# First stage of an attention and two-layer feed-forward kernel: pooled sums by TensorE, another split of one value load, another program order

## The chip, the cores and the metric

The kernel runs on one core of a Trainium2 chip. The metric is the device time of one execution in microseconds (us). Before the change it is 943.6 us, the median of three runs (943.38 to 944.88). The execution that was profiled took 947.2 us.

## What is computed

Inputs are `q`, `k`, `v` of shape (4, 8, 576, 64) in float32 and four weight matrices in float64. Cut to what matters:

```python
q_d, k_d, v_d = means of 4 neighbouring rows (576 -> 144 rows)
out_d = softmax(q_d @ k_d.T / 8) @ v_d             # pooled attention, each row used 4 times
scores = q @ k.T / 8, only where |i - j| < 4       # local attention, 7 keys for a query
out = repeat(out_d, 4) + softmax(scores) @ v       # then to (2304, 512)
h = x @ w_in;  x = (h - tanh(h)) @ w_out           # 512 -> 2048 -> 512
h = x @ w_in2; out = (h * cos(h)) @ w_out2
```

## The kernel before, in words

The 2304 tokens are cut into chunks: rows 0 to 511 of each of the four batches are one chunk of 512 tokens, the last 64 rows of all batches together are one of 256. The second batch's chunk is taken as two halves of 256 tokens ("second chunk" below is the first half). The first feed-forward layer runs chunk by chunk (`ffn1`): sixteen steps, in each twelve matmuls x @ w_in (L744) and, two steps later, twelve matmuls with w_out (L764). The second layer follows with all five chunks. Each factor of a matmul is held as a high and a low half, so a product is three matmuls.

The weights come as float64 and are turned into float32 pairs on the chip. This is one *tick* of the class `Weights`: two ScalarE steps (L121, L123), one VectorE step (L127), a copy for the high half (GpSimd for the first three pieces, ScalarE then) and a GpSimd subtraction for the low half (L142). Each tick also issues the load of a further piece on SP, into a buffer that an earlier tick's VectorE step gives free. The first chunk needs 32 pieces, two for each of its sixteen steps.

There are two kinds of attention. The first chunk's is written for TensorE (`first_attention`): keys and queries are loaded in four tiles of 128 rows each (`load_nat`), transposed (`tr`), and from the transposed tiles VectorE makes the sums of four neighbours (`red`). The same is done for the last 64 rows of all batches (`load_lo`, `tr_l`, 'left-over' rows). Local scores are worked in eight blocks of 64 queries: scores (`b_s`), maximum, subtraction and exponential (`b_m`), sum and division (`b_n`), transposition (`b_t`), then products with the values (`b_v`) and the low half of the result (`b_l`). A value block is 70 rows (`load_vw`); the first begins three rows ahead of the sequence. The pooled attention runs in four pairs of heads (`P.s`, `P.e`, `P.n`, `P.t`, `P.t2`, `P.v`); the sums of its values are `vsum` on GpSimd. After nearly every TensorE step a matmul on zeros is issued (`warm`, L359).

The other chunks' local attention (`attention`) is elementwise: GpSimd multiplies (L553 for queries with keys, L602 for values), VectorE reduces. Their pooled attention shares the class `Pooled`; its keys need a copy of left-over rows on GpSimd (L261).

Order. Every step of the attention and every tick is an event with a key (a time in a plan). The events up to `T0` are written out in the order of their keys, and each engine works its instructions in just this order. After `T0` the events are handed out along the feed-forward loop (5.2 units of the plan for a step of a 512-token chunk), and a planner arranges the instructions. `TB` is the plan time at which the second chunk's attention begins, `TL` the earliest of its loads, `TS` the distance of two of its products. Weight ticks stand at `TE + 2.3 * i` for the first `KE` and after that from `T0` on at a distance of `TW`. In the plan before the first stage's steps have fixed distances: tiles every 2.5, score blocks every 3.1, pooled pairs every 2.2; six ticks and three products of the second chunk lie among the stage's last steps.

Of the kernel before, what the change touches and what calls it, by code (L numbers as in the profile page):

```python
# [27 lines left out]
def kernel(  # L28
# [11 lines left out]
    nc = tc.nc  # L40
# [18 lines left out]
    def pool(name, bufs=1, **kw):  # L59
        return tc.tile_pool(name=name, bufs=bufs, **kw)  # L60
# [5 lines left out]
    ps_h = ctx.enter_context(pool("ps_h", 2, space=PS))  # L66
    ps_a = ctx.enter_context(pool("ps_a", 2, space=PS))
# [5 lines left out]
    lp = st_lp.enter_context(pool("lp"))  # L73
# [91 lines left out]
    ident = ao.tile([128, 128], F32, name="ident")  # L165
# [3 lines left out]
    klq = cst.tile([128, 2, NP, 64], F32, name="klq")  # L169
    vl = cst.tile([128, DM], F32, name="vl")  # L170
# [159 lines left out]
    def first_attention(ch):  # L330
# [37 lines left out]
        def rows_of(src, b, t0, n):  # L368
            return src[b, :, t0:t0 + n, :].rearrange("h s d -> s h d")
# [16 lines left out]
        def load_vw(i):  # L386
            t = lp.tile([NK, H, D], F32, tag="g", name="vw", bufs=12)
            G["vw", i] = t
            a0 = NQ * i - (R - 1)
            z = max(0, -a0)  # L390
            nc.sync.dma_start(out=t[z:NK], in_=rows_of(v, 0, a0 + z, NK - z))
            if z:
                nc.sync.dma_start(out=t[0:z], in_=rows_of(v, 0, 0, z))

        def masks():
            nc.vector.memset(zero, 0.0)
            nc.gpsimd.memset(mask, 0.0)
# [12 lines left out]
            warm(10)  # L410

        def turn_nat(g):
            a = ps_a.tile([128, NP, 128], F32, tag="a", name="pa_tr")
            for u in range(NP):
                nc.tensor.transpose(a[:, u, :], g[:, 2 * u:2 * u + 2, :].rearrange("p e d -> p (e d)"), ident)
            return a

        def tr(nm, t):
            a = turn_nat(G.pop((nm, t)))
            if nm == "q":  # L420
                nc.scalar.activation(qT[:, :, 128 * t:128 * t + 128], a, AF.Copy, scale=0.125)
            else:
                nc.vector.tensor_copy(kT[:, :, R - 1 + 128 * t:R - 1 + 128 * t + 128], a)

        def red(nm, t):
            src, w, o, dst = (qT, 512, 0, qd) if nm == "q" else (kT, 512 + 2 * (R - 1), R - 1, kd)
            nc.vector.tensor_reduce(out=dst[:, :, 32 * t:32 * t + 32],
                                    in_=view(src, [[w, NP], [R, 32], [1, R]], off=o + 128 * t), axis=AX.X, op=ALU.add)

        def tr_l(nm, j):  # L430
            a = turn_nat(G.pop((nm, "l", j)))
            nc.vector.tensor_reduce(out=klq[:, 0 if nm == "k" else 1, :, 32 * j:32 * j + 32],
                                    in_=view(a, [[128, NP], [R, 32], [1, R]]), axis=AX.X, op=ALU.add)
            if (nm, j) == ("k", 0):
                nc.vector.tensor_copy(kT[:, :, 512 + R - 1:512 + 2 * (R - 1)], a[:, :, 0:R - 1])
            if nm == "q":
                ql = klq[:, 1, :, 32 * j:32 * j + 32]
                nc.scalar.activation(ql, ql, AF.Copy, scale=0.125 / (R * R))

        def pooled_qk():  # L440
# [72 lines left out]
        for t in range(NT_):
            keyed += [(0.1 + 0.01 * t, (load_nat, "k", t)), (0.105 + 0.01 * t, (load_nat, "q", t))]
            keyed += [(4.6 + 2.5 * t, (tr, "k", t)), (5.6 + 2.5 * t, (red, "k", t)), (5.8 + 2.5 * t, (tr, "q", t)), (7.2 + 2.5 * t, (red, "q", t))]
        keyed += [(14.7, (tr_l, "k", 0)), (15.9, (tr_l, "q", 0)), (16.8, pooled_qk), (32.0, (tr_l, "k", 1)), (32.9, (tr_l, "q", 1))]
        keyed += [(19.0 + 0.6 * n, x) for n, x in enumerate(vsums)]
        for u in range(NP):
            t0 = 17.4 + 2.2 * u
            keyed += [(t0 + dt, (fn, u)) for dt, fn in ((0, P.s), (1.3, P.e), (3.9, P.n), (5.5, P.t), (6.7, P.t2))]  # L520
            keyed += [(max(t0 + 8.4, 23.0 + 2.4 * u), (P.v, u))]
        for i in range(NB):
            t0 = 8.1 + 3.1 * i
            keyed += [(0.4 + 0.01 * i, (load_vw, i))]
            keyed += [(t0 + dt, (fn, i)) for dt, fn in ((0, b_s), (1.2, b_m), (3.7, b_n), (6.0, b_t))]
        for j in range(NB // 2):
            keyed += [(33.2 + 1.8 * j, (b_v, j)), (35.1 + 1.8 * j, (b_l, j))]
# [282 lines left out]
    W1, W2 = Weights(w_in1, w_out1), Weights(w_in2, w_out2)  # L810
# [174 lines left out]
```

## Time and profile before

| | |
|---|---|
| median of three runs | 943.6 us |
| profiled execution | 947.2 us |
| its span | 945.4 us |
| TensorE busy | 905.0 us, 96% |
| VectorE busy | 577.9 us, 61% |
| ScalarE busy | 480.6 us, 51% |
| GpSimd busy | 402.7 us, 43% |
| mean granted TensorE clock | 0.981 |

Engines in the rows: PE is TensorE, PEld its weight loads, DVE VectorE, ACT ScalarE, POOL GpSimd, SP SyncE, which issues most of the loads. A timeline row gives start and length in us, engine, source line, operation, output and inputs, the count of merged instructions, and in brackets how long the engine stood idle before it and what ended that. Matmuls are pipelined, so lengths overlap and starts are the better measure.

### The profile page before, as it was taken

How to read it: one execution, taken by the hardware profiler on the slowest of the kernel's cores; microseconds unless marked ns; L12 is line 12 of the kernel's file. 1: busy time of each engine (PE TensorE's matmuls, PEld its weight loads, DVE VectorE, ACT ScalarE, POOL GpSimd, SP SyncE). 2: the span in 40 equal slices, each digit the busy share in tenths (PEclk: the TensorE clock that was granted, in tenths of full speed). 3: DMA queues.
4: the chain of work that ended last, by engine and by line, in shares of the span. 5: the costliest groups of instructions: out<-in, count | busy, mean ns of one | idle time of the engine just before them, and what ended most of it. 6: DMA issues, size and time to landing. Idle time of an engine off the chain costs nothing.

```text
span 945.4 us, 13574 instructions
## 1 busy us (share of the span) xinstructions
PE 905.0 (96%) x4922; PEld 748.9 (79%) x4930; DVE 577.9 (61%) x964; ACT 480.6 (51%) x1012; POOL 402.7 (43%) x432
## 2 busy tenths in 40 slices
PE   7859999799998999999999989999999999999997
PEld 4537777599997777778889968888888888888896
DVE  6588777888879862663225576546545554545463
ACT  3658786333433344274227886535544454445464
POOL 3579899889888871540004533101111111111010
PEclk9979999799999999999999999999999999999999
DMA  9688654522323131172014731010101010100000
GB/s 179 120 270 306 218 172 135 159 79 87 98 93 98 40 94 35 34 226 87 1 62 133 227 118 64 1 45 0 45 1 45 1 45 0 45 23 1 23 23 23
DMA packets 65939, 81.73 MB, mean 86 GB/s; under 512 B 21966, under 2 KB 46548, under 8 KB 65872
## 3 DMA queue, kind: packets, MB, share of 16 engines
q1 hardware_dynamic: 64544, 76.01, 27.2%
q0 software_dynamic: 1232, 4.72, 1.5%
q8 instruction: 39, 0.64, 0.3%
q14 instruction: 28, 0.23, 0.1%
q10 hardware_dynamic: 96, 0.13, 0.1%
HBM read 71.40 MB, written 9.44 MB: 86 GB/s over the span
## 4 chain that ended last, share of the span: by engine, by line
PE 73%; DVE 8%; ACT 8%; DMA 6%; issue 2%; POOL 2%; ACTq 0%; DVEq 0%; POOLq 0%
PE h L744 35%; PE oacc L901 21%; PE acc L764 14%; DMA raw<-in_moe_w_out_dram 4%; DMA raw<-in_moe_w_in_dram 2%; DVE wf L127 1%; ACT raw L123 1%; ACT pe L280 1%; DVE o L606 1%; ACT wp L121 1%; PE pa_x L639 1%; DMA qt<-in_q_dram 1%; PE pa_s L269 1%; POOL pr L602 1%; ACT wf L121 1%
## 5 line engine op out<-in xcount | busy, mean ns | idle before, releaser
L901 PE MATMUL oacc<-o,i 128*128 128x512 f32 x864 | 209.8, 392 | 3.3 <-ACT i L751 2.7
L744 PE MATMUL h<-xh,i 128*128 128x512 f32 (+1 forms) x768 | 206.8, 346 | 1.7 <-ACT xh L498 1.6
L764 PE MATMUL acc<-gh,o 128*128 128x512 f32 (+1 forms) x768 | 200.9, 342 | 5.7 <-ACT gh L755 5.7
L744 PE MATMUL h<-x2h,i 128*128 128x512 f32 (+1 forms) x640 | 193.2, 369 | 0.0
L901 PEld LDWEIGHTS oacc<-o,i 128*128 128x128 f32 x864 | 160.8, 188 | 39.3 <-ACT i L751 4.0
L916 POOL TENSOR_SCALAR y<-y 128x512 f32<-128x512 f32 (+1 forms) x80 | 46.8, 584 | 327.9 <-ACT y L914 315.4
L744 PEld LDWEIGHTS h<-xh,i 128*128 128x128 f32 x768 | 137.0, 195 | 19.1 <-issue 2.5
L764 PEld LDWEIGHTS acc<-gh,o 128*128 128x128 f32 x768 | 133.5, 190 | 23.2 <-ACT gh L755 7.3
L744 PE MATMUL h<-xl,i 128*128 128x512 f32 (+1 forms) x384 | 133.1, 347 | 3.5 <-DVE xl L502 3.3
L553 POOL TENSOR_TENSOR pr<-qt,kt 128x896 f32<-128x896 f32 x56 | 119.5, 2145 | 36.1 <-DVE o L606 30.0
L744 PEld LDWEIGHTS h<-x2h,i 128*128 128x128 f32 x640 | 116.7, 188 | 21.7
L764 PE MATMUL acc<-gl,o 128*128 128x512 f32 (+1 forms) x384 | 129.2, 339 | 0.2 <-DVE gl L790 0.2
L744 PE MATMUL h<-x2l,i 128*128 128x512 f32 (+1 forms) x320 | 118.0, 369 | 0.0
L602 POOL TENSOR_TENSOR pr<-vt,s 128x896 f32<-128x896 f32 x56 | 105.2, 1930 | 3.8 <-DVE o L606 1.4
L921 DVE TENSOR_TENSOR h<-h,rr 128x512 f32<-128x512 f32 (+1 forms) x80 | 51.6, 645 | 83.4 <-ACT rr L920 83.1
L919 ACT ACTIVATE rr<-rr 128x512 f32<-128x512 f32 (+1 forms) x80 | 47.1, 588 | 100.7 <-DVE rr L918 100.7
L744 PEld LDWEIGHTS h<-xl,i 128*128 128x128 f32 x384 | 74.7, 195 | 12.2 <-DVE xl L502 4.1
L923 DVE TENSOR_TENSOR i<-h,i 128x512 fp32r<-128x512 f32 (+1 forms) x80 | 50.7, 634 | 48.4 <-ACT i L751 48.3
L764 PEld LDWEIGHTS acc<-gl,o 128*128 128x128 f32 x384 | 72.8, 190 | 8.3 <-DVE gl L790 0.7
L788 DVE TENSOR_TENSOR h<-h,th 128x512 f32<-128x512 f32 x72 | 49.8, 694 | 47.0 <-ACT th L787 46.6
L787 ACT ACTIVATE th<-h 128x512 f32<-128x512 f32 x72 | 42.7, 595 | 66.3 <-PE h L744 66.1
L755 ACT ACTIVATE gh<-h 128x512 fp32r<-128x512 f32 x72 | 42.8, 594 | 65.8 <-PE acc L764 51.8
(171 smaller groups left out, 1243.9 us busy)
## 6 DMA issues: line engine op xcount, KB each, us to landing
raw<-in_moe_w_in_dram SPq DMA_DIRECT2D x32, 512.0 KB
raw<-in_moe_w_out_dram SPq DMA_DIRECT2D x32, 512.0 KB
kt<-in_k_dram SPq DMA_DIRECT2D x16, 320.0 KB
vt<-in_v_dram SPq DMA_DIRECT2D x16, 320.0 KB
kt<-in_k_dram SPq DMA_DIRECT2D x16, 256.0 KB
vt<-in_v_dram SPq DMA_DIRECT2D x16, 256.0 KB
x2l<-x2d POOLq DMA_DIRECT2D x4, 1024.0 KB, 5.6
out_dram<-os SPq DMA_DIRECT2D x16, 256.0 KB
```

The source lines that it names most:

```text
L553: nc.gpsimd.tensor_tensor(out=pr.rearrange("p j f d -> p j (f d)"), in0=view(L["q", h], [[0, OFF], [1, 2 * D]], off=f * D), in1=view(L["k" ...
L602: nc.gpsimd.tensor_tensor(out=pr.rearrange("p f d j -> p j f d"), in0=view(L["v", h], [[D, OFF], [D, 2], [1, D]], off=f * D), in1=view(L[" ...
L744: nc.tensor.matmul(hp[:, i * n:i * n + n], lhsT=wt[:, kk * 128:(kk + 1) * 128], rhs=xt, start=(c == 0), stop=(c == 3 * KD - 1))
L755: nc.scalar.activation(gh, hp, AF.Copy)
L764: nc.tensor.matmul(acc[e], lhsT=wt[:, e * 128:(e + 1) * 128], rhs=gt, start=(f == 0 and i == 0), stop=(f == KF - 1 and i == 2))
L787: it = nc.scalar.activation(th, hp, AF.Tanh)
L788: nc.vector.tensor_tensor(out=hp, in0=hp, in1=th, op=ALU.subtract)
L901: nc.tensor.matmul(acc[t], lhsT=gt[:, t * 128:(t + 1) * 128], rhs=wt, start=(g == 0 and a_ == 0), stop=(g == KF - 1 and a_ == 2))
L916: ip = nc.gpsimd.tensor_scalar(out=y, in0=y, scalar1=-ROUND, scalar2=-TWO_PI_HI, op0=ALU.add, op1=ALU.mult)
L919: nc.scalar.activation(r, r, AF.Abs)
L921: nc.vector.tensor_tensor(out=hp, in0=hp, in1=r, op=ALU.mult)
L923: nc.vector.tensor_tensor(out=G[f][1], in0=hp, in1=G[f][0].bitcast(F32), op=ALU.subtract)
```

## The change

- The sums of four neighbours of keys and queries are made by TensorE, from the tiles as loaded, with a 128 x 32 matrix of ones (`pmat`); VectorE's reductions of the transposed tiles go. The left-over tiles are no longer transposed: the same product gives their sums, with three more columns where three left-over keys are needed as they are.
- The first value block is loaded as 64 + 3 + 3 rows instead of 67 + 3.
- Every step of the first stage has a key of its own. Key and query tiles come in the order 0, 3, 1, 2 and 0, 3, 2, 1; score blocks in the order 0, 4, 1, 2, 3, 5, 7, 6.
- `T0`, `TB`, `TL`, `TS` and `TW` get other values, and two ticks instead of six lie before `T0`.

```diff
+        pmat = lp.tile([128, 32 + R - 1], F32, name="pmat")
...
-            z = max(0, -a0)
-            nc.sync.dma_start(out=t[z:NK], in_=rows_of(v, 0, a0 + z, NK - z))
-            if z:
-                nc.sync.dma_start(out=t[0:z], in_=rows_of(v, 0, 0, z))
+            if a0 >= 0:
+                nc.sync.dma_start(out=t, in_=rows_of(v, 0, a0, NK))
+                return
+            nc.sync.dma_start(out=t[NK - 64:NK], in_=rows_of(v, 0, a0 + NK - 64, 64))
+            for z in (0, R - 1):
+                nc.sync.dma_start(out=t[z:z + R - 1], in_=rows_of(v, 0, 0, R - 1))
...
+            nc.gpsimd.memset(pmat, 1.0)
+            nc.gpsimd.affine_select(out=pmat[:, 0:32], in_=pmat[:, 0:32], compare_op=ALU.is_ge, fill=0.0, base=0,
+                                    pattern=[[-R, 32]], channel_multiplier=1)
+            nc.gpsimd.affine_select(out=pmat[:, 0:32], in_=pmat[:, 0:32], compare_op=ALU.is_ge, fill=0.0, base=R - 1,
+                                    pattern=[[R, 32]], channel_multiplier=-1)
+            nc.gpsimd.tensor_copy(pmat[:, 32:32 + R - 1], ident[:, 0:R - 1])
...
         def tr(nm, t):
-            a = turn_nat(G.pop((nm, t)))
+            g = pairs(G.pop((nm, t)))
+            a = ps_a.tile([128, NP, 128], F32, tag="a", name="pa_tr")
+            for u in range(NP):
+                nc.tensor.transpose(a[:, u, :], g[u], ident)
+            if t == 0:
+                G["p" + nm] = ps_h.tile([128, NP, 128], F32, tag="h", name="pa_p" + nm)
+            for u in range(NP):
+                nc.tensor.matmul(G["p" + nm][:, u, 32 * t:32 * t + 32], lhsT=g[u], rhs=pmat[:, 0:32])
...
-        def red(nm, t):
-            src, w, o, dst = (qT, 512, 0, qd) if nm == "q" else (kT, 512 + 2 * (R - 1), R - 1, kd)
-            nc.vector.tensor_reduce(out=dst[:, :, 32 * t:32 * t + 32],
-                                    in_=view(src, [[w, NP], [R, 32], [1, R]], off=o + 128 * t), axis=AX.X, op=ALU.add)
-
         def tr_l(nm, j):
-            a = turn_nat(G.pop((nm, "l", j)))
-            nc.vector.tensor_reduce(out=klq[:, 0 if nm == "k" else 1, :, 32 * j:32 * j + 32],
-                                    in_=view(a, [[128, NP], [R, 32], [1, R]]), axis=AX.X, op=ALU.add)
+            g = pairs(G.pop((nm, "l", j)))
+            w = 32 + (R - 1) * ((nm, j) == ("k", 0))
+            a = ps_a.tile([128, NP, 128], F32, tag="a", name="pa_trl")
+            for u in range(NP):
+                nc.tensor.matmul(a[:, u, 0:w], lhsT=g[u], rhs=pmat[:, 0:w])
+            if nm == "k":
+                nc.vector.tensor_copy(klq[:, 0, :, 32 * j:32 * j + 32], a[:, :, 0:32])
+            else:
+                nc.scalar.activation(klq[:, 1, :, 32 * j:32 * j + 32], a[:, :, 0:32], AF.Copy, scale=0.125 / (R * R))
...
+        def pooled_k():
+            nc.vector.tensor_copy(kd[:, :, 0:128], G["pk"])
+            nc.gpsimd.tensor_copy(kd[:, :, 128:SG], klq[:, 0, :, 0:LG])
+
+        def pooled_q():
             for e in range(2):
-                nc.scalar.activation(qz[64 * e:64 * e + 64, :, e, :], qd[64 * e:64 * e + 64], AF.Copy, scale=1.0 / (R * R))
+                nc.scalar.activation(qz[64 * e:64 * e + 64, :, e, :], G["pq"][64 * e:64 * e + 64], AF.Copy, scale=0.125 / (R * R))
...
+        keyed = [(-11.11, masks), (-3.58, load_vl), (-2.55, load_vg), (12.23, pooled_q), (14.53, pooled_k), (16.07, load_w)]
+        for fn, nm, ts in (
+                (load_nat, "k", (-27.69, -18.48, -13.36, -19.69)),
+                (load_nat, "q", (-22.4, -10.64, -11.95, -19.31)),
+                (tr, "k", (-11.1, -4.77, 2.45, -8.41)),
+                (tr, "q", (-6.77, 12.12, 7.3, 11.27)),
+                (load_lo, "k", (-3.77, 6.14)),
+                (load_lo, "q", (-6.83, 0.2)),
+                (tr_l, "k", (13.57, 18.81)),
+                (tr_l, "q", (12.22, 24.25)),
...
+                (load_vw, (18, 12.74, 20.51, 8.04, 14.62, 13.87, 2.35, 14.22)),
+                (P.s, (15.3, 16.14, 19.35, 18.3)),
...
+                (P.v, (19.75, 22.51, 27.14, 27.35)),
+                (b_s, (2.69, 14, 16.43, 16.46, 13.22, 20.14, 20.68, 18.44)),
+                (b_m, (12.11, 15.29, 17.52, 19.3, 13.42, 20.16, 22.88, 24.57)),
+                (b_n, (12.13, 17.82, 18.12, 19.36, 16.13, 20.25, 26.44, 25.67)),
...
+                (b_v, (28.77, 29.17, 30.06, 31.28)),
+                (b_l, (30.05, 30.87, 31.42, 31.43)),
...
-    T0, TB, TL = 41.0, 34.0, 31.0
-    TS, TS_POOL, TW = 2.5, 0.9, 1.4
+    T0, TB, TL = 43.42, 38.81, 34.91
+    TS, TS_POOL, TW = 2.57, 0.9, 2.28
...
-    TE, KE = 28.5, 6
+    TE, TD, KE = 27.16, 2.17, 2
...
-        events.append((TE + 2.3 * i if i < KE else T0 + 0.3 + TW * (i - KE), 0, lambda: W1.tick(raw_a, nc.gpsimd)))
+        events.append((TE + TD * i if i < KE else T0 + 0.3 + TW * (i - KE), 0, lambda: W1.tick(raw_a, nc.gpsimd)))
```

## Rows read from the trace of the kernel before

**Rows 1.** Busy time by stage: stretch, its length, then each engine's busy us (instructions)
```profile
0.00:20.00 20.00, 15.97 (x122) 9.97 (x124) 13.20 (x29) 6.02 (x11) 6.84 (x25) 1.00 1.13 201
20.00:40.00 20.00, 16.43 (x138) 10.74 (x139) 9.90 (x31) 10.96 (x39) 13.99 (x29) 0.91 0.73 137
40.00:60.00 20.00, 15.44 (x206) 10.12 (x206) 14.79 (x32) 12.54 (x32) 10.75 (x9) 1.00 0.61 181
60.00:80.00 20.00, 11.90 (x50) 8.28 (x51) 17.91 (x32) 13.24 (x28) 16.11 (x15) 0.66 0.93 316
80.00:171.00 91.00, 90.61 (x420) 70.92 (x418) 68.84 (x119) 65.62 (x151) 83.36 (x83) 1.00 0.60 189
```
**Rows 2.** Timeline of TensorE where the first chunk's feed-forward matmuls begin
```profile
65.26 1.19 PE L744 MATMUL h<-xh,i 128*128 128x512 f32 x2 [1.59 <-ACT xh L498]
69.79 0.79 PE L744 MATMUL h<-xl,i 128*128 128x512 f32 x1 [3.34 <-DVE xl L502]
...
79.17 0.97 PE L269 MATMUL pa_s<-kT,qz 128*128 128x144 f32 x6 [2.12 <-DVE wf L127]
```
**Rows 3.** Timeline of TensorE between the first chunk's last matmul and the second's first
```profile
173.03 0.39 PE L764 MATMUL acc<-gh,o 128*128 128x512 f32 x1
...
180.56 0.78 PE L744 MATMUL h<-xh,i 128*128 128x256 f32 x2
```
**Rows 4.** Timeline of GpSimd: first product, products beside weight low halves, a pooled copy
```profile
54.44 2.08 POOL L553 TENSOR_TENSOR pr<-qt,kt 128x896 f32<-128x896 f32 x1 [0.63 <-DMA kt<-in_k_dram]
...
125.87 2.13 POOL L553 TENSOR_TENSOR pr<-qt,kt 128x896 f32<-128x896 f32 x1
127.95 1.32 POOL L142 TENSOR_TENSOR i<-wf,i 128x512 fp32r<-128x512 f32 x1
129.20 2.16 POOL L553 TENSOR_TENSOR pr<-qt,kt 128x896 f32<-128x896 f32 x1
...
150.99 0.52 POOL L261 COPY qz<-klq 64x64 f32<-64x64 f32 x2
```
**Rows 5.** VectorE's groups, 0 to 62 us: busy, mean ns, idle before and its releaser
```profile
L127 DVE SCALAR_TENSOR_TENSOR wf<-wf,raw 128x512 uint32<-128x512 uint32 x5 | 4.3, 852 | 2.3 <-ACT raw L123 2.3
...
L432 DVE TENSOR_REDUCE klq<-pa_tr 128x128 f32<-128x512 f32 x4 | 2.8, 689 | 1.8 <-PE pa_tr L415 1.8
...
L427 DVE TENSOR_REDUCE kd<-kTn 128x128 f32<-128x512 f32 x4 | 2.7, 680 | 0.0
L427 DVE TENSOR_REDUCE qd<-qT 128x128 f32<-128x512 f32 x4 | 2.7, 678 | 0.4 <-ACT qT L421 0.4
...
L495 DVE TENSOR_TENSOR pa_o<-pa_o,up 128x512 f32<-128x512 f32 x3 | 2.1, 690 | 0.1
...
L502 DVE TENSOR_TENSOR xl<-pa_o,xh 128x512 fp32r<-128x512 f32 x2 | 1.4, 683 | 0.6 <-ACT xh L498 0.6
```
**Rows 6.** TensorE's groups, 0 to 62 us
```profile
L359 PE MATMUL idle<-zero 128*128 128x512 bf16 x50 | 20.5, 447 | 1.2 <-DVE zero L396 1.2
L456 PE MATMUL cs<-kTn,qT 64*64 64x70 f32 x128 | 6.1, 239 | 0.0
...
L415 PE MATMUL pa_tr<-ident,kg 128*128 128x128 f32 x16 | 2.6, 290 | 0.0
```
**Rows 7.** Timeline of SP, which issues the loads
```profile
15.52 12.62 SPq L393 DMA_DIRECT2D vw<-in_v_dram  x1
...
47.70 0.43 SPq L218 DMA_DIRECT2D qt<-in_q_dram  x1
```
**Rows 8.** DMA in one stretch: length, TensorE clock, mean share of 16 engines, GB/s
```profile
22.00:27.00 5.00, 0.66 0.11 20
```
**Rows 9.** Timeline of ScalarE at its first weight piece
```profile
43.46 0.65 ACT L121 ACTIVATE wf<-raw 128x512 f32<-128x512 f32 x1
```
**Rows 10.** GpSimd's weight low halves, 54 to 186 us
```profile
L142 POOL TENSOR_TENSOR o<-wf,o 128x512 fp32r<-128x512 f32 x16 | 20.9, 1308 | 1.3 <-ACT o L135 1.1
L142 POOL TENSOR_TENSOR i<-wf,i 128x512 fp32r<-128x512 f32 x14 | 18.3, 1304 | 0.2
```

More of the change, by code (lines that the diff above doesn't have):

```diff
@@ L340, in first_attention @@
         kT = lp.tile([128, NP, 512 + 2 * (R - 1)], F32, name="kTn")
-        qd = lp.tile([128, NP, 128], F32, name="qd")
         kd = lp.tile([128, NP, SG], F32, name="kd")
@@ L389, in load_vw, with load_vl, load_w @@
             a0 = NQ * i - (R - 1)
-            z = max(0, -a0)
-            nc.sync.dma_start(out=t[z:NK], in_=rows_of(v, 0, a0 + z, NK - z))
-            if z:
-                nc.sync.dma_start(out=t[0:z], in_=rows_of(v, 0, 0, z))
+            if a0 >= 0:
[4 more added lines that the diff above has]
+                nc.sync.dma_start(out=t[z:z + R - 1], in_=rows_of(v, 0, 0, R - 1))
+        def load_vl():
+            G["vl"] = lo_load(v)
+        def load_w():
+            W1.load(raw_a, 2)
         def masks():
             nc.vector.memset(zero, 0.0)
+            nc.gpsimd.memset(pmat, 1.0)
[4 more added lines that the diff above has]
+            nc.gpsimd.tensor_copy(pmat[:, 32:32 + R - 1], ident[:, 0:R - 1])
             nc.gpsimd.memset(mask, 0.0)
@@ L410, in masks, with pairs, tr @@
             warm(10)
-        def turn_nat(g):
+        def pairs(g):
+            return [g[:, 2 * u:2 * u + 2, :].rearrange("p e d -> p (e d)") for u in range(NP)]
+        def tr(nm, t):
+            g = pairs(G.pop((nm, t)))
             a = ps_a.tile([128, NP, 128], F32, tag="a", name="pa_tr")
             for u in range(NP):
-                nc.tensor.transpose(a[:, u, :], g[:, 2 * u:2 * u + 2, :].rearrange("p e d -> p (e d)"), ident)
-            return a
-        def tr(nm, t):
-            a = turn_nat(G.pop((nm, t)))
+                nc.tensor.transpose(a[:, u, :], g[u], ident)
[3 more added lines that the diff above has]
+                nc.tensor.matmul(G["p" + nm][:, u, 32 * t:32 * t + 32], lhsT=g[u], rhs=pmat[:, 0:32])
             if nm == "q":
@@ L423, in tr @@
                 nc.vector.tensor_copy(kT[:, :, R - 1 + 128 * t:R - 1 + 128 * t + 128], a)
-        def red(nm, t):
-            src, w, o, dst = (qT, 512, 0, qd) if nm == "q" else (kT, 512 + 2 * (R - 1), R - 1, kd)
-            nc.vector.tensor_reduce(out=dst[:, :, 32 * t:32 * t + 32],
-                                    in_=view(src, [[w, NP], [R, 32], [1, R]], off=o + 128 * t), axis=AX.X, op=ALU.add)
         def tr_l(nm, j):
-            a = turn_nat(G.pop((nm, "l", j)))
-            nc.vector.tensor_reduce(out=klq[:, 0 if nm == "k" else 1, :, 32 * j:32 * j + 32],
-                                    in_=view(a, [[128, NP], [R, 32], [1, R]]), axis=AX.X, op=ALU.add)
-            if (nm, j) == ("k", 0):
[L435 to L440, printed above, removed]
+            g = pairs(G.pop((nm, "l", j)))
[7 more added lines that the diff above has]
+                nc.scalar.activation(klq[:, 1, :, 32 * j:32 * j + 32], a[:, :, 0:32], AF.Copy, scale=0.125 / (R * R))
+            if (nm, j) == ("k", 0):
+                nc.vector.tensor_copy(kT[:, :, 512 + R - 1:512 + 2 * (R - 1)], a[:, :, 32:w])
+        def pooled_k():
+            nc.vector.tensor_copy(kd[:, :, 0:128], G["pk"])
+            nc.gpsimd.tensor_copy(kd[:, :, 128:SG], klq[:, 0, :, 0:LG])
+        def pooled_q():
             for e in range(2):
-                nc.scalar.activation(qz[64 * e:64 * e + 64, :, e, :], qd[64 * e:64 * e + 64], AF.Copy, scale=1.0 / (R * R))
-            nc.gpsimd.tensor_copy(kd[:, :, 128:SG], klq[:, 0, :, 0:LG])
+                nc.scalar.activation(qz[64 * e:64 * e + 64, :, e, :], G["pq"][64 * e:64 * e + 64], AF.Copy, scale=0.125 / (R * R))
             for u in range(NP):
@@ L506, in vsum @@
             sum_rows(o[:, 128 * u:128 * u + 128], G[nm][:, 2 * u:2 * u + 2])
-        vsums = [(vsum, o_, nm, u) for u in range(NP) for o_, nm in ((vd, "vg"), (vl, "vl"))]
         with_pe = (tr, tr_l, P.s, P.t, P.t2, P.v, b_s, b_t, b_v)
-        keyed = [(0.0, masks), (0.15, (load_lo, "k", 0)), (0.16, (load_lo, "q", 0)), (0.2, load_vg),
-                 (0.3, lambda: G.update(vl=lo_load(v))), (0.6, lambda: W1.load(raw_a, 2)),
-                 (0.7, (load_lo, "k", 1)), (0.8, (load_lo, "q", 1))]
@@ L513, in first_attention @@
[L513 to L527, printed above, removed]
+        keyed = [(-11.11, masks), (-3.58, load_vl), (-2.55, load_vg), (12.23, pooled_q), (14.53, pooled_k), (16.07, load_w)]
[8 more added lines that the diff above has]
+                (tr_l, "q", (12.22, 24.25)),
+        ):
+            keyed += [(t, (fn, nm, i)) for i, t in enumerate(ts)]
@@ new lines, in first_attention @@
+        for fn, ts in (
+                (load_vw, (18, 12.74, 20.51, 8.04, 14.62, 13.87, 2.35, 14.22)),
+                (P.s, (15.3, 16.14, 19.35, 18.3)),
+                (P.e, (17.02, 18.39, 19.39, 19.17)),
+                (P.n, (17.03, 20.15, 20.84, 21.43)),
+                (P.t, (17.88, 21.59, 20.85, 26.68)),
+                (P.t2, (19.25, 21.8, 24.04, 26.69)),
+                (P.v, (19.75, 22.51, 27.14, 27.35)),
+                (b_s, (2.69, 14, 16.43, 16.46, 13.22, 20.14, 20.68, 18.44)),
+                (b_m, (12.11, 15.29, 17.52, 19.3, 13.42, 20.16, 22.88, 24.57)),
+                (b_n, (12.13, 17.82, 18.12, 19.36, 16.13, 20.25, 26.44, 25.67)),
+                (b_t, (13.75, 18.43, 20.02, 27.39, 17.7, 25.52, 29.91, 30.09)),
+                (b_v, (28.77, 29.17, 30.06, 31.28)),
+                (b_l, (30.05, 30.87, 31.42, 31.43)),
+        ):
+            keyed += [(t, (fn, i)) for i, t in enumerate(ts)]
@@ L528, in first_attention @@
+        for nm, o_, ts in (("vg", vd, (17.17, 15.81, 17.53, 20.24)), ("vl", vl, (18.27, 20.3, 14.65, 19.58))):
+            keyed += [(t, (vsum, o_, nm, u)) for u, t in enumerate(ts)]
         for t, fn in keyed:
```

## The prediction

> **What bounds the kernel now.** I read the busy table by stage first, because a share over the whole span hides the start. From 80 us on TensorE is busy nearly without a gap (90.61 of 91 us to 171 us), and before that it is not: 11.90 of 20 us between 60 and 80, at a granted clock of 0.66 [rows 1]. So the end is set by when the feed-forward matmuls begin, and by what interrupts them later.
>
> Second, TensorE in order of time. The first feed-forward matmul (L744) starts at 65.26 us, the next one waits until 69.79 for the last low half of the first chunk (L502), and a last hole ends at 79.17 behind a weight half (L127) [rows 2]. From there to the last matmul of the first chunk at 173.03 nothing is lost. Then the second chunk is not ready: its first matmul comes at 180.56 [rows 3].
>
> Third, GpSimd, which builds the second chunk. Its first product starts at 54.44, when the keys of that chunk land, and from then on products and weight low halves (L142) alternate, a product and a half taking 3.33 us (125.87 to 129.20); the copy for the fourth pooled pair of that chunk is reached only at 150.99 [rows 4]. GpSimd is busy 83.36 of the 91 us up to 171 [rows 1]. The first two stages thus have two limits: the first stage sets when TensorE starts, and GpSimd sets when the second chunk is ready.
>
> **The change, part by part.** *Pooled sums on TensorE.* VectorE loses the eight reductions of L427 (2.7 + 2.7 us) and the four of L432 (2.8) [rows 5] and gains one 512-element copy (0.7, as one of L495) and two 128-element copies (0.5 together): 7.0 us less. TensorE gains four matmuls of 32 columns in each of eight tiles. No row shows these; an fp32 matmul of 70 columns is 6.1 / 128 = 0.05 us an instruction and comes as two, which gives 0.4 us a tile, and four transposes of 128 columns are 2.6 / 4 = 0.65 [rows 6]. I take 0.4, the row nearer in columns, 3 us in all (5 at the other end). Its cover is that 20.5 us of TensorE's busy time before 62 us are matmuls on zeros [rows 6]; without that cover it would delay the first scores by 1 or 2 us, which I keep in the range. The matrix of ones costs GpSimd a fill, two selections and a copy, about 1 us ahead of the masks; what it delays is the first scores, which in the new order stand behind four transposed tiles anyway: nothing.
>
> *The values of the first block.* SP sits 12.62 us on the issue behind the 67-row load (15.52 to 28.14) [rows 7], while all DMA engines together run at a share of 0.11 and 20 GB/s [rows 8]. Queued behind it are the other value blocks, the first two weight loads and the left-over keys and queries. But ScalarE reaches the first weight only at 43.46, with no wait shown [rows 9]: it gets there late in its own program order. So I price the removal at nothing in the old order; in the new one it lets the weights land in time. The two more three-row loads cost SP an issue each (0.43 us, as the one at 47.70 [rows 7]). On SP the left-over keys and queries now stand ahead of the values, the two weight loads behind five value blocks, and from the thirteenth tile of twelve buffers on each load waits for an earlier tile's transposes; all of it has until about 40 us, when ScalarE comes to the weights, and costs nothing there. The Trainium skill, "DMA: Bandwidth & Descriptors", section "Why a DMA increments its semaphore by 16 and not by 1", says that a transfer is spread over the largest count up to 16 that divides its slowest dimension, so 67 rows go through one engine and 64 through sixteen. The low share agrees. If that stall were itself on the path the sum would be 12.6 us better than below; the ScalarE row says it is not.
>
> *The order.* VectorE is busy 13.20 + 9.90 + 14.79 = 37.9 us before 60 us [rows 1]. The new stage has 7.0 less, and three of the five weight steps of L127 go behind it (3 x 0.85 = 2.6); one addition of L495 (0.7) and two subtractions of L502 (1.4) that come after 60 us now are added [rows 5]: 29.4 us. Today VectorE works 37.9 of the 55 us after its first 5 us (0.69), in the worst 20 us 0.50, in the best 0.74 [rows 1]. In the new order two to three score blocks are open at once, where the old one held them at a fixed distance, and neither products of the second chunk nor four of the weight ticks stand between. At 0.69 the stage takes 43 us and ends at 48; at 0.74 it ends at 45, at 0.50 at 64. The first block's scores now wait behind three key tiles, a start some 2 us later. I take **50 us** for the last low half, against 69.8: TensorE could start almost 20 us sooner.
>
> *What is late next.* The second chunk's loads follow, on SP, the weight load of the second tick, which waits for that tick's VectorE step. In the old order the chunk's first load is issued at 47.70 [rows 7] and the first product follows at 54.44, 6.7 us later. In the new order the second tick stands some 6 us before the stage's end, so at 44; with fewer transfers beside it the first product comes 5 us later, at 49 (48 to 54): GpSimd starts **5.4 us** sooner, not 20. Moving work out of its way gives more: today 30 low halves follow the first product, and all but the last stand in front of the copy for the fourth pair [rows 10]. By the new constants that copy stands at 38.81 + 56.3 = 95.1, where 2 + (95.1 - 43.72) / 2.28, about 25, ticks have been placed, one of them still open: 24 halves, five fewer. At 1.3 us each [rows 10] that is 6.5 us. So the copy moves from 150.99 by 12 us to 139, and if the rest of the chain to the second chunk's first matmul keeps its length (180.56 - 150.99 = 29.6), that matmul comes at 168.6.
>
> The same spacing slows TensorE. The fourth weight half, which the second multiply needs, is done after three products and four halves: 49 + 3 x 2.1 + 4 x 1.3 = 60.5. From then on each half shares GpSimd with 2.28 / 2.57 = 0.89 products: 1.25 + 0.89 x 2.08 (both are steps in [rows 4]), with 0.3 for the small ones, 3.4 us. Twenty-eight halves take 95 us, and the last twelve matmuls 2.7: the first chunk ends at 158, against 173.42 (173.03 + 0.39), 15 us sooner. TensorE at its present pace would need 92 us from there and end at 153. Both chains, 12 and 15 us, end close together. After this boundary I move everything by the same amount; that no later stage gives a part back is not shown by these rows and is left to the range.
>
> **The sum.** The profiled execution took 947.2 us, 945.4 in the span and 1.8 around it. Less 14.5 it becomes 932.7. The median of the runs is 943.6, 3.6 below the profiled one, so the forecast is **929 us**; its own range is 924 to 934.
>
> **The rivals.** (a) *The second chunk takes only GpSimd's earlier start.* If the auto-ordered part keeps its weight halves ahead of the products, the 6.5 us do not come and the boundary moves by 5.4: 938. For it: matmuls need the halves and pull them forward on demand. Against it: the ticks stand in program order and are spread.
> (b) *Both chains are shorter.* If the 29.6 us behind the copy are mostly TensorE's own queue, which now runs 20 us ahead, TensorE alone is the limit and the second chunk starts at 153: 27.6 us, 916. For it: that chain contains transposes and products queued behind the feed-forward matmuls. Against it: GpSimd's load.
> (c) *Slower: the first chunk starves for weights.* Two ticks instead of six are done when the stage ends, and GpSimd works in order: a low half that waits for its ScalarE and VectorE steps holds the products, and a product holds the next half. The matmuls lose when a half takes over (180.56 - 2.7 - 60.5) / 28 = 4.2 us. At 4.5 the first chunk ends at 189, 8 us late: 952. For it: the L142 group already waits on ScalarE for 1.1 us [rows 10]. Against it: the present pairs run at 3.33.
> (d) *The new order does not shorten the stage.* With VectorE at its worst share the stage ends at 64, 6 us sooner, and the slower weight pace eats that: no change, 943.6.
>
> **How the numbers follow.** Forecast 0.42, (a) 0.18, (b) 0.24, (c) 0.11, (d) 0.05. A measurement of this kernel tells about 0.2%, 1.9 us, from no change. Faster is the forecast, (a), (b) and a fifth of (d): 0.85; within 0.2% most of (d): 0.04; slower 0.11. The range reaches down past (b) by the 5 us that a stage end of 45 instead of 50 would add, to 911, and up to no change, 944; outside stand (c) and the tail of (b). Where the likeliest case is wanted alone, 924 to 934 stands beside it.
>
> **What would show it.** In the changed profile: the group of L427 gone from VectorE and its busy time before the first feed-forward matmul near 29 us; no SP issue over 3 us among the value loads; the last low half of the first chunk near 50 us; the first product of the second chunk near 49; weight halves on GpSimd 3.4 us apart; the first chunk's last matmul near 158 and the second chunk's first near 166 to 169. The forecast is wrong if the first product comes with the stage's old end (above 54), if halves are over 4.2 us apart, or if the second chunk's first matmul directly follows the first chunk's last.

## The result and the profile after

The changed kernel takes 928.9 us in the median (927.3 to 930.2) against 943.5 for the kernel before in the same comparison: a ratio of 0.9841, 95% interval 0.982 to 0.9862. The profiled execution took 927.9 us, span 926.2, against 947.2 [table of before]; the profiled pair thus differs by 19.3 us (its spans by 19.2), the medians by 14.7.

Busy time by stage, as in [rows 1], and one more stretch around the first chunk's end, first for the kernel before and then for the changed one:

```profile
160.00:200.00 40.00, 33.80 (x196) 27.22 (x196) 34.61 (x61) 15.61 (x49) 34.43 (x32) 0.87 0.47 146
```
```profile
0.00:20.00 20.00, 18.65 (x157) 15.00 (x160) 5.30 (x12) 6.21 (x12) 7.68 (x30) 1.00 0.99 215
20.00:40.00 20.00, 19.47 (x202) 14.07 (x206) 15.47 (x48) 11.72 (x41) 14.73 (x30) 1.00 0.55 134
40.00:60.00 20.00, 16.57 (x200) 10.95 (x204) 11.47 (x24) 12.83 (x30) 7.81 (x7) 0.90 0.45 146
60.00:80.00 20.00, 18.87 (x80) 15.36 (x81) 19.31 (x37) 15.34 (x34) 14.60 (x16) 0.93 0.98 341
80.00:171.00 91.00, 88.26 (x427) 67.63 (x427) 70.09 (x125) 69.46 (x163) 83.47 (x85) 1.00 0.60 187
...
160.00:200.00 40.00, 39.79 (x303) 37.03 (x302) 35.92 (x64) 17.73 (x48) 34.85 (x28) 1.00 0.42 129
```

TensorE gains 7 us of busy time between 60 and 80 us, loses 2.4 between 80 and 171, where it now has small waits (88.26 against 90.61), and gains 6 at the boundary, where the granted clock is 1.00 instead of 0.87 as well: 303 matmuls instead of 196 between 160 and 200 us (the second chunk's are only 256 columns wide, so the count overstates the work). The timeline of TensorE in the changed kernel shows both ends, to be read against [rows 2, 3]:

```profile
58.73 1.19 PE L774 MATMUL h<-xh,i 128*128 128x512 f32 x2 [0.98 <-POOL pr L583]
59.79 0.79 PE L774 MATMUL h<-xl,i 128*128 128x512 f32 x1
...
158.35 0.49 PE L321 MATMUL pa_v<-pt,vd 128*64 128x160 f32 x4
159.83 0.49 PE L324 MATMUL pa_v<-pe,vl 16*64 16x160 f32 x4 [0.99 <-ACT pe L313]
...
166.34 0.40 PE L774 MATMUL h<-xh,i 128*128 128x256 f32 x2
...
168.20 1.09 PE L794 MATMUL acc<-gh,o 128*128 128x512 f32 x4
```

The first feed-forward matmul comes 6.5 us sooner and the low halves hold nothing up. At the far end the second chunk's first matmul (166.34) stands ahead of the first chunk's last ones, which end at 169.3: no hole is left. By the start of the first copy that closes a chunk, 5.6 us are won by the first chunk's end (174.2 to 168.7), 18.7 by the second's (238.7 to 220.0), and 18 to 19 stay to the end.

GpSimd, against [rows 4] and [rows 10]: the timeline, then the view of one line's instructions from 56 us on, with two earlier halves left out (count, shortest, median and longest ns, first and last start).

```profile
56.50 4.14 POOL L583 TENSOR_TENSOR pr<-qt,kt 128x896 f32<-128x896 f32 x2 [0.40 <-DMA kt<-in_k_dram]
...
61.84 1.28 POOL L142 TENSOR_TENSOR i<-wf,i 128x512 fp32r<-128x512 f32 x1
...
122.92 0.52 POOL L261 COPY qz<-klq 64x64 f32<-64x64 f32 x2
...
146.75 0.54 POOL L261 COPY qz<-klq 64x64 f32<-64x64 f32 x2
```
```profile
L142 POOL TENSOR_TENSOR o<-wf,o x16: 1277/1298/1318, 60.6 to 164.4; 128x512 fp32r<-128x512 f32 x16
L142 POOL TENSOR_TENSOR i<-wf,i x14: 1275/1294/1317, 61.8 to 149.4; 128x512 fp32r<-128x512 f32 x14
```

Each copy of L261 follows the scores of the pair before it (one `qz` buffer), so the fourth pair's is the one at 122.92; that at 146.75 belongs to the next half. Before, 31 low halves and 22 products stood in front of the fourth pair's copy (150.99); now 19 and 16 do. The halves themselves last until 164.40 + 1.3.

### The profile page after: what moved, and what is told of

It reads as the page before. It is cut to its first block, busy times and chain, and to the rows that moved or that the text cites. A ratio compares the mean times of both kernels' runs of the same rounds, so it can differ in the third digit from the quotient of the medians.

```text
span 926.2 us, 13703 instructions
## 1 busy us (share of the span) xinstructions
PE 903.2 (98%) x5001; PEld 752.4 (81%) x5010; DVE 570.9 (62%) x955; ACT 480.2 (52%) x1012; POOL 401.7 (43%) x436
## 4 chain that ended last, share of the span: by engine, by line
PE 83%; DVE 6%; ACT 5%; DMA 5%; issue 1%; POOL 0%; SPq 0%; ACTq 0%; POOLq 0%
PE h L774 37%; PE oacc L931 21%; PE acc L794 17%; DMA raw<-in_moe_w_in_dram 3%; DVE wf L127 1%; PE idle L359 1%; DMA raw<-in_moe_w_out_dram 1%; ACT raw L123 1%; PE pa_s L269 1%; PE pa_x L669 1%; ACT wf L121 1%; PE pa_t L296 1%; PE pa_v L324 1%; PE pa_v L321 1%; PE cs L475 1%
## 5 line engine op out<-in xcount | busy, mean ns | idle before, releaser
L794 PE MATMUL acc<-gh,o 128*128 128x512 f32 (+1 forms) x768 | 198.3, 342 | 6.4 <-ACT gh L785 5.6
L774 PEld LDWEIGHTS h<-xh,i 128*128 128x128 f32 x768 | 135.0, 192 | 21.2 <-POOL pr L583 1.7
L794 PE MATMUL acc<-gl,o 128*128 128x512 f32 (+1 forms) x384 | 127.3, 337 | 0.0
```

What stands on the lines that cost most here:

```text
L774: nc.tensor.matmul(hp[:, i * n:i * n + n], lhsT=wt[:, kk * 128:(kk + 1) * 128], rhs=xt, start=(c == 0), stop=(c == 3 * KD - 1))
L794: nc.tensor.matmul(acc[e], lhsT=wt[:, e * 128:(e + 1) * 128], rhs=gt, start=(f == 0 and i == 0), stop=(f == KF - 1 and i == 2))
```

## The experiments

All ratios are to the kernel before on the same chip, with the 95% interval; its medians were 943.5 to 947.1, so the ratios compare better than the times. Times in the table are read from the timelines: the end of the last matmul of the first chunk, the start of the products with pooled values (`pa_v`) of the second chunk's fourth pair, that chunk's first feed-forward matmul, and the copies that close it.

| kernel | us | ratio | first chunk ends | 4th `pa_v` | second starts | ends |
|---|---|---|---|---|---|---|
| before | 943.5 | 1 | 173.4 | 177.6 | 180.6 | 238.7 |
| after | 928.9 | 0.984 | 169.3 | 158.4 | 166.3 | 220.0 |
| b_split | 945.5 | 1.000 | 171.7 | 175.6 | 178.5 | 236.2 |
| b_sums | 957.6 | 1.011 | 178.1 | 184.1 | 187.0 | 248.0 |
| b_plan | 951.1 | 1.006 | 189.4 | 178.6 | 184.6 | 243.3 |
| a_oldplan | 944.6 | 0.999 | 164.9 | 173.8 | 176.6 | 237.3 |
| v_oldplan | 945.6 | 0.998 | 166.8 | 174.7 | 177.9 | 236.9 |
| a_67 | 928.8 | 0.981 | 170.0 | 159.1 | 167.1 | 220.7 |
| a_vsums | 929.9 | 0.982 | 166.8 | 156.7 | 163.8 | 217.4 |
| a_tw14 | 938.1 | 0.991 | 160.4 | 167.1 | 171.0 | 230.8 |
| a_tw19 | 935.6 | 0.989 | 165.3 | 165.2 | 168.1 | 226.8 |
| a_tw27 | 936.2 | 0.989 | 174.2 | 151.7 | 169.7 | 227.3 |
| v_tw20 | 936.3 | 0.989 | 163.6 | 163.5 | 167.1 | 226.0 |
| a_te20 | 942.1 | 0.995 | 178.5 | 170.1 | 176.3 | 232.9 |

**b_split**: the kernel before with the new split of the load alone.

```diff
...
-            nc.sync.dma_start(out=t[z:NK], in_=rows_of(v, 0, a0 + z, NK - z))
...
+            nc.sync.dma_start(out=t[NK - 64:NK], in_=rows_of(v, 0, a0 + NK - 64, 64))
+            for z in (0, R - 1):
+                nc.sync.dma_start(out=t[z:z + R - 1], in_=rows_of(v, 0, 0, R - 1))
```

> The kernel before with only the first value block loaded as 64 + 3 + 3 rows. My theory: the 12.6 us for which SP stood behind the 67-row load go, but ScalarE comes to the first weight only at 43.5 us in its own order, so the time stays at 942 to 945. Rival (the stalled queue was the cost): the weights start earlier and the time falls by 6 to 12 us, to 932 to 938.

0.9999 (0.9986 to 1.0013): no change, as the theory said; 945.5 lies above its 942 to 945 only as the kernel before does in this comparison (945.7). The timeline of SP in this kernel has the long issue of [rows 7] gone, and the time did not follow:

```profile
14.97 0.75 SPq L393 DMA_DIRECT2D vw<-in_v_dram  x1
15.76 0.84 SPq L395 DMA_DIRECT2D vw<-in_v_dram  x2
```

**b_sums**: the kernel before with the sums on TensorE, in the old order and plan.

```diff
+                nc.tensor.matmul(G["p" + nm][:, u, 32 * t:32 * t + 32], lhsT=g[u], rhs=pmat[:, 0:32])
...
-            keyed += [... (5.6 + 2.5 * t, (red, "k", t)), ... (7.2 + 2.5 * t, (red, "q", t))]
-        keyed += [... (16.8, pooled_qk) ...]
+        keyed += [... (16.8, pooled_q), (16.81, pooled_k) ...]
```

> The kernel before with only the sums of four neighbours moved from VectorE to TensorE, in the old order and plan. My theory: 7 us less on VectorE, most of it before 21 us where VectorE has almost no holes, but the stage's later part is paced by the waits between VectorE and ScalarE and by the weight ticks; at most 3 us reach the second chunk's start: 940 to 944. Rival (VectorE's work is the stage's limit): all 5 to 7 us arrive, 936 to 939.

Slower, 1.011 (1.0079 to 1.0142): both expectations fell. The timeline of TensorE in this kernel:

```profile
18.36 0.60 PE L425 MATMUL pa_tr<-ident,qg 128*128 128x128 f32 x4
18.79 0.98 PE L429 MATMUL pa_pq<-pmat,qg 128*128 128x32 f32 x8
19.61 0.38 PE L359 MATMUL idle<-zero 128*128 128x512 bf16 x1
...
28.36 1.81 PE L269 MATMUL pa_s<-kd,qz 128*128 128x144 f32 x6 [3.19 <-POOL kd L450]
```

A tile's sums take 0.82 us (18.79 to 19.61), and the matmul on zeros behind them is issued all the same. The first pooled scores come at 28.36, before at 21.70, after a wait of 3.19 us for a GpSimd copy of left-over keys. How the 12 us of the whole divide among the sums and such waits is not shown.

**b_plan**: the kernel before with the six new plan constants alone.

```diff
-    T0, TB, TL = 41.0, 34.0, 31.0
-    TS, TS_POOL, TW = 2.5, 0.9, 1.4
+    T0, TB, TL = 43.42, 38.81, 34.91
+    TS, TS_POOL, TW = 2.57, 0.9, 2.28
-    TE, KE = 28.5, 6
+    TE, TD, KE = 27.16, 2.17, 2
...
```

> The kernel before with only the six plan constants changed (T0, TB, TL, TS, TW and two ticks instead of six before T0); sums, split and the first stage's order are the old ones. My theory: the hole between the first and the second chunk (173.4 to 180.6 us and the slow clock behind it) goes because fewer weight halves stand in front of the second chunk's products, and the first stage ends sooner with four ticks less in it; 930 to 938. Rival (the new order of the first stage does it): 942 to 946, or slower because the first chunk waits for weights.

1.0059 (1.0037 to 1.0081), slower, as the rival said: the first chunk ends 16 us later, at 189.4, and TensorE is idle 7.1 us between 80 and 189.4. That weights are the reason is shown in part only: by the view of its waits TensorE waited 1.3 us there for a weight half and 5.8 for the second chunk's pooled pairs.

**a_oldplan**: the changed kernel with the old constants (the diff of b_plan backwards).

```diff
...
-    TS, TS_POOL, TW = 2.57, 0.9, 2.28
+    TS, TS_POOL, TW = 2.5, 0.9, 1.4
-    TE, TD, KE = 27.16, 2.17, 2
+    TE, TD, KE = 28.5, 2.3, 6
```

> The changed kernel with the six plan constants of before (ticks every 1.4, six of them before T0). My theory: the first stage's own steps still end early, but ticks and products lie among its last steps again and the hole before the second chunk returns in part; 934 to 941. Rival (the order of the first stage does it alone): 927 to 931.

0.9985 (0.9972 to 0.9998): the direction was right, the size not; practically the whole gain is gone, although the first chunk ends at 164.9, 8.5 us sooner than before. **v_oldplan** takes the sums off as well:

```diff
...
+                (red, "k", (-11.095, -4.765, 2.455, -8.405)),
+                (red, "q", (-6.765, 12.224, 12.222, 12.223)),
...
-    TS, TS_POOL, TW = 2.57, 0.9, 2.28
+    TS, TS_POOL, TW = 2.5, 0.9, 1.4
...
```

> The first stage's new program order and the 64 + 3 + 3 load alone: sums on VectorE as before, and the six plan constants of before. Theory (order without the new distances gains nothing at the first boundary): 941 to 946. Rival (the order alone is worth 5 us or more, and it was the sums on TensorE that took it in the kernel with the old plan): 935 to 940.

0.9984 (0.9967 to 1.0001), as the theory said. The order gains next to nothing alone, the constants lose alone, and together they gain 1.6%.

**a_67** and **a_vsums**: the changed kernel with the 67-row load, and with VectorE's sums.

```diff
...
-            nc.sync.dma_start(out=t[NK - 64:NK], in_=rows_of(v, 0, a0 + NK - 64, 64))
-            for z in (0, R - 1):
-                nc.sync.dma_start(out=t[z:z + R - 1], in_=rows_of(v, 0, 0, R - 1))
+            nc.sync.dma_start(out=t[z:NK], in_=rows_of(v, 0, a0 + z, NK - z))
+            if z:
+                nc.sync.dma_start(out=t[0:z], in_=rows_of(v, 0, 0, z))
```

> The changed kernel with the first value block again as 67 + 3 rows. In the new order that block stands behind the two weight loads on SP, and SP's next load waits for a tick's VectorE step at 48 us anyway, so a stall of 12 us from 28 to 41 us meets nobody. My theory: 927 to 931. Rival (the split is part of the gain): 933 or more.

```diff
-                nc.tensor.matmul(G["p" + nm][:, u, 32 * t:32 * t + 32], lhsT=g[u], rhs=pmat[:, 0:32])
...
+        def red(nm, t):
...
+            nc.vector.tensor_reduce(out=dst[:, :, 32 * t:32 * t + 32], ...)
```

> The changed kernel with the sums of four neighbours on VectorE again, from the transposed tiles, in the new order and plan. In the changed kernel TensorE has no hole from 5 to 23 us: the sums of a tile take 0.82 us there, and VectorE is busy 5.3 of the first 20 us. My theory now: TensorE's sums delay the first stage, without them it ends 3 to 6 us sooner, and since GpSimd and the weights hang on its end the time falls to 922 to 927. Rival (VectorE's seven us are what the change saved): 931 to 936.

0.9811 (0.9795 to 0.9826) and 0.9816 (0.9793 to 0.9839): neither part carries the gain. Without the sums on TensorE the stage ends 3.8 us sooner (last low half 55.28, not 59.05) and the second chunk 2.5, but the median does not follow; the theory's 922 to 927 is not borne out, and the rival's 931 to 936 is refuted.

**a_tw14, a_tw19, a_tw27**: the changed kernel with another distance of the weight ticks, 1.4 (shown), 1.9 and 2.7; **v_tw20** is a_vsums with 2.05.

```diff
-    TS, TS_POOL, TW = 2.57, 0.9, 2.28
+    TS, TS_POOL, TW = 2.57, 0.9, 1.4
```

> The changed kernel with weight ticks every 1.4 after T0 instead of 2.28, still two before T0. My theory: GpSimd takes the weight halves first, so the first chunk's matmuls are no longer held (its end near 160 instead of 169 us) but the fourth pooled pair of the second chunk is late again and a hole of 8 to 12 us opens before it: 934 to 941. Rival (the fewer ticks before T0 matter, not the spacing): 927 to 931.

> The changed kernel with TW = 1.9 instead of 2.28, nothing else. Theory (the gain is bought with the distance of the weight ticks, in proportion): with 1.4 the time was 938.1, with 2.28 928.9, so 1.9 gives about 933 (931 to 935), and the second chunk's first 256-wide matmul comes near 168.5. Rival (a threshold: it is enough that the second chunk is ready before the first one ends): 927 to 930.

> The changed kernel with TW = 2.7 instead of 2.28, nothing else. Theory (beyond some distance the first chunk starves): a half then shares GpSimd with 2.7 / 2.57 = 1.05 products, 1.25 + 1.05 x 2.08 + 0.3 = 3.7 us, 28 halves last 104.6 instead of 97.2, the first chunk ends near 176 and the time is 7 us longer, 933 to 938. Rival (TensorE fills the waits with matmuls of the second chunk, which is ready sooner still): 926 to 930.

> The changed kernel with the sums on VectorE again, as in a_vsums, and TW = 2.05. Theory: a_vsums had its stage 3.7 us sooner than the changed kernel but spent that on waiting for weight halves; with a shorter distance the first chunk ends some 6 us sooner while the second chunk comes 3 us later, and the time is 925 to 929. Rival (the distance 2.28 is already where the two chains meet): 930 to 934.

Ratios 0.9914 (0.989 to 0.994), 0.9887 (0.9869 to 0.9905), 0.9891 (0.9874 to 0.9907) and 0.989 (0.9875 to 0.9904). The theories on the changed kernel held (a_tw19 is 0.6 us above its bound, in a comparison whose kernel before was 2.7 us above the first one's); for v_tw20 the theory fell, and the rival's direction held but not its 930 to 934. Of the distances tried 2.28 is the best, with a loss on both sides. Busy times for 1.4, 1.9 and 2.7 in turn:

```profile
80.00:160.00 80.00, 79.76 (x371) 62.23 (x370) 60.23 (x104) 62.63 (x141) 74.15 (x72) 1.00 0.61 192
160.00:200.00 40.00, 31.49 (x212) 27.14 (x211) 33.45 (x59) 14.57 (x44) 34.88 (x35) 0.83 0.45 144
```
```profile
80.00:160.00 80.00, 78.87 (x367) 61.20 (x366) 59.03 (x105) 64.50 (x146) 71.54 (x74) 1.00 0.61 194
160.00:200.00 40.00, 35.31 (x249) 31.20 (x248) 35.80 (x61) 16.51 (x45) 36.94 (x30) 0.96 0.47 142
```
```profile
80.00:160.00 80.00, 73.03 (x343) 54.77 (x342) 56.38 (x101) 62.18 (x146) 71.28 (x74) 1.00 0.62 193
160.00:200.00 40.00, 39.16 (x271) 35.27 (x269) 35.48 (x61) 18.00 (x43) 36.53 (x30) 1.00 0.48 148
```

Short distances keep TensorE full until 160 and leave it idle and at a lower clock behind; the long one takes 7 us in front of the boundary and 0.8 behind it. With 1.4 the hole lies where the kernel before had one: the fourth pair's scores, its transposes after a wait, its products with values.

```profile
160.21 0.90 PE L269 MATMUL pa_s<-kT,qz 128*128 128x144 f32 x6
165.19 1.12 PE L296 MATMUL pa_t<-ident,pe 128*128 128x128 f32 x4 [4.08 <-ACT pe L290]
...
167.13 0.80 PE L321 MATMUL pa_v<-pt,vd 128*64 128x160 f32 x4 [0.42 <-ACT pt L304]
```

The table shows the two chains cross: from 1.4 to 2.7 the first chunk ends later and later (160.4, 165.3, 169.3, 174.2), the fourth pair comes sooner and sooner (167.1, 165.2, 158.4, 151.7).

**a_te20**: the changed kernel with its two early ticks at 20.27 and 22.44 of the plan.

```diff
-    TE, TD, KE = 27.16, 2.17, 2
+    TE, TD, KE = 20.27, 2.17, 2
```

> The changed kernel with its two early ticks at 20.27 and 22.44 instead of 27.16 and 29.33. GpSimd stands idle from 38 to 48 us and the third weight piece, loaded only after the first tick, holds ScalarE at 53 us in front of the last two score blocks. My theory: the ticks fit into ScalarE's holes between 34 and 44 us, the third piece has landed when it is needed, the second chunk's loads are issued some 8 us sooner and the stage ends 2 to 4 us sooner: 922 to 927. Rival (ScalarE is the stage's chain there): each tick's 1.1 to 2.2 us lengthen the stage, 929 to 934.

0.995 (0.9934 to 0.9965): both fell. GpSimd's timeline shows one reason: it works in order, and a weight's high-half copy that waits for VectorE stands in front of the divisions (L287) of two pooled pairs.

```profile
40.58 0.61 POOL L133 CAST i<-wf 128x512 fp32r<-128x512 f32 x1 [5.53 <-DVE wf L127]
...
42.80 0.91 POOL L287 TENSOR_TENSOR pe<-pe,pr__565 128x432 f32<-128x432 f32 x1
```

TensorE waits 5.33 us for them, up to 43.76, and starts its feed-forward matmuls at 69.08, 10.4 us later than the changed kernel. The other half of these 10.4 us was not traced.

## Why the prediction came out right, and which of its steps did not

The time was forecast at 929 and is 928.9. The kind of gain (an earlier start, and weight steps out of GpSimd's way, so that two chains end close together) is confirmed; several sizes were wrong and cancelled, and that the figures agree so closely is luck.

Two things show it. The sum takes 14.5 us off, which the working before it does not give: the later of its two chains, the second chunk from 180.56 to 168.6, moves by 12.0, and that makes 931.6. And of the three signs that were to show the forecast wrong, two came: the first product is at 56.5 (the sign was above 54), and the second chunk's first matmul follows the first chunk's work without a hole. The third, halves over 4.2 us apart, did not. Of what was to confirm it, the reductions of L427 are gone and the second chunk's first matmul is inside its 166 to 169; the stage's end, the first product, the pace of the halves and the first chunk's end are not where they were put, and SP sits 3.88 us on one value load (at 15.07), where none over 3 was to be.

*The sums, 0.4 us a tile under cover: wrong.* Columns were the wrong measure; the row that gave 0.05 us an instruction has a 64 x 64 stationary tile, these have 128 x 128. TensorE's timeline of the changed kernel, against [rows 6]:

```profile
5.12 0.60 PE L433 MATMUL pa_tr<-ident,kg 128*128 128x128 f32 x4
5.55 0.98 PE L437 MATMUL pa_pk<-pmat,kg 128*128 128x32 f32 x8
6.37 0.38 PE L359 MATMUL idle<-zero 128*128 128x512 bf16 x1
```

A tile's sums take 0.82 us. The matmuls on zeros are not cover: they stand in program order between the steps, so the sums come on top, and a_vsums has its stage end 3.8 us sooner.

*Stage end at 50: it was 59.7, the step that failed by most.* Besides the sums there is a wait that the working did not have. ScalarE's timeline:

```profile
53.36 0.67 ACT L121 ACTIVATE wf<-raw 128x512 f32<-128x512 f32 x1 [1.59 <-DMA raw<-in_moe_w_in_dram]
53.93 0.65 ACT L123 ACTIVATE raw<-raw 128x512 uint32<-128x512 uint16 x1
54.48 0.58 ACT L501 ACTIVATE cp<-cpt 70x512 f32<-70x512 f32 x1
...
55.43 0.59 ACT L501 ACTIVATE cp<-cpt 70x512 f32<-70x512 f32 x1
```

The third weight piece, behind its load, stands ahead of the last two copies that the local output needs. VectorE's busy time before 60 us is 32.2, not 29.4, and its share of the time 0.59, not 0.69. That is below the working share taken from the old order; the bound of 0.50, which gave 64, was the nearer one. Of the 9.7 us between 50 and 59.7, a_vsums shows 3.8 for the sums, and the wait with the two weight steps behind it takes 2.7 (up to 54.48); the rest stays open.

*First product at 49: 56.5.* The second chunk's first load is issued at 52.20 instead of 44, as it hangs on the second tick, which is late with the stage. GpSimd starts 2.1 us later than before, so rival (a), which rests on an earlier start, has no ground. The 5.4 us of the sum did not come.

*Five fewer halves, copy at 139: too small.* Twelve fewer, and six products fewer, stand in front of it; 12 x 1.3 + 6 x 2.1 = 28, and it comes at 122.92. Why so many fewer, the runs do not show. *The tail of 29.6 us is kept: wrong the other way*, 43.4 (122.92 to 166.34). The fourth pair's own transposition (`pa_qk`) and scores (`pa_s`), first before and then in the changed kernel:

```profile
162.57 0.44 PE L632 MATMUL pa_qk<-ident,qkd 128*128 128x128 f32 x2
...
167.87 0.90 PE L269 MATMUL pa_s<-kT,qz 128*128 128x144 f32 x6
```
```profile
139.38 0.38 PE L662 MATMUL pa_qk<-ident,qkd 128*128 128x128 f32 x2
...
142.81 0.90 PE L269 MATMUL pa_s<-kT,qz 128*128 128x144 f32 x6
```

Of the 13.8 us more, 4.9 lie ahead of the transposition, 5.8 between the scores and the products with values (`pa_v`, in the table), 5.0 behind those, where TensorE works on the first chunk; the step from transposition to scores is 1.9 shorter. The net, second chunk at 168.6, was 166.34.

*Halves 3.4 us apart, first chunk at 158: mis-sized by 11 us.* The fourth half is done at 61.84 + 1.3 = 63.1, not 60.5, and the 28 after it take 102.6 us, 3.66 each. What was counted does give 3.4; what was left out are GpSimd's own waits from 63 to 166 us (the view of waits: for whom, in all, times, longest):

```profile
POOL i L142 <- ACT i L135: 2.8, 3, 1.0
POOL o L142 <- ACT o L135: 2.4, 2, 1.7
POOL r L616 <- DVE r L612: 2.2, 2, 1.7
```

So the first chunk ends at 63.1 + 102.6 + 3.6 = 169.3. But TensorE's own queue ends almost there too. Its first matmul with w_out, before and in the changed kernel, and its busy time from there to the first chunk's end, before, changed and a_tw14:

```profile
79.89 1.19 PE L764 MATMUL acc<-gh,o 128*128 128x512 f32 x4
```
```profile
67.79 1.20 PE L794 MATMUL acc<-gh,o 128*128 128x512 f32 x4 [1.13 <-ACT gh L785]
```
```profile
79.90:173.40 93.50, 92.88 (x428) 72.45 (x427) 71.34 (x123) 66.16 (x153) 85.66 (x86) 1.00 0.59 187
```
```profile
67.80:169.30 101.50, 98.76 (x468) 76.13 (x469) 80.57 (x145) 78.79 (x186) 91.38 (x92) 1.00 0.64 204
```
```profile
67.70:160.40 92.70, 92.46 (x428) 72.86 (x429) 71.98 (x126) 74.55 (x169) 84.00 (x83) 1.00 0.66 214
```

With the halves out of the way (a_tw14) TensorE needs 92.7 us, the 92 of the prediction, but counted from 67.7 and not from 60.5: it ends at 160.4, and rival (b)'s 153 was out of reach. In the changed kernel it takes 8.8 us more, of which 2.5 are idle time; the rest is 40 more matmuls, work of the second chunk that is done ahead (its fourth pooled pair, its transpositions and 14 of its first feed-forward matmuls). So the slow halves cost little and the 11 us were no loss. Rival (c) had the slower halves, but its point of 4.2 us a half is not reached. Rival (d) had the start about right (6 us sooner; it is 6.5) and missed that the second chunk comes sooner.

*Nothing from the split: right*, in the old order and in the new (b_split, a_67).

*Everything after the boundary moves alike: wrong.* 14.2 us were won at the second chunk's first matmul and 18.7 at its end. The kernel before had this behind its hole:

```profile
180.00:185.00 5.00, 4.29 (x19) 4.00 (x20) 4.10 (x9) 1.22 (x5) 3.98 (x2) 0.50 0.60 189
185.00:190.00 5.00, 4.24 (x28) 3.77 (x27) 5.00 (x10) 1.46 (x6) 4.80 (x6) 0.83 0.30 91
```

Behind the hole TensorE was at a granted clock of 0.50, the 1.2 GHz level; in the changed kernel it is at 1.00 from 160 to 200 us. It also stood idle more of the time until the second chunk's end, 2.4 of 58.1 us before and 0.2 of 53.7 now:

```profile
180.60:238.70 58.10, 55.67 (x433) 53.15 (x432) 51.58 (x89) 20.92 (x60) 51.20 (x42) 0.95 0.30 93
```
```profile
166.30:220.00 53.70, 53.49 (x436) 51.51 (x436) 48.76 (x84) 22.42 (x63) 47.94 (x42) 1.00 0.37 113
```

The profiled execution so came 4.8 us below the forecast 932.7. The median did not: the offset of 3.6 us between profile and median, carried over from before, is -1.0 for the changed kernel. Why these offsets differ, and why the medians give 14.7 where the profiles give 19.3, stays open.

Shown by the runs: the gain needs the new order and the new constants together (b_plan, a_oldplan, v_oldplan). The order starts TensorE sooner (12.1 us at its first matmul with w_out). Of this 4.1 us are left at the first chunk's end and about 2 go to waits; the rest goes to work of the second chunk, which the slower weights let GpSimd bring forward, so that it is ready when the first ends. Of the constants only `TW` and `TE` were varied by themselves: `TW` back at 1.4 gives up about half of the gain (0.991), and what `T0`, `TB`, `TL`, `TS` and the number of early ticks are worth one by one is not shown. No variant tried beats the changed kernel beyond the uncertainty.

## What to carry to other kernels

Where two chains meet at a boundary, a constant that feeds one at the other's expense can have a narrow best value: mark the end of both chains and move it until they meet. Look also at what the busy engine does in the time that it seems to lose; here it was work brought forward. Count the work that stands in front of a marker on an in-order engine, in both kernels, before pricing what is moved past it. Fillers that stand in program order between the steps are no cover for more work on that engine. And a forecast that comes true is checked by its steps, not by its total.

## What the runs showed of the hardware

An fp32 product of a 128 x 128 stationary tile with 32 columns goes as two instructions of 0.10 us each (eight in 0.82 us), about as long as a transpose of 128 columns (four in 0.43 us, 5.12 to 5.55): per instruction, fewer columns bought nothing here. With a 64 x 64 stationary tile and 70 columns an instruction took 0.05 us [rows 6].
